# A fused attention and two-FFN kernel: the first token tile takes one chunk of each of the four batches instead of four chunks in a row, and its state products are issued after the first FFN products

## The chip, the core and the metric

The kernel runs on one core of a Trainium2 chip. The core has five engines with a queue each, and each queue is worked off in order: TensorE (PE: matmuls, and PEld, its weight loads), VectorE (DVE), ScalarE (ACT), GpSimd (POOL) and SyncE (SP). In this kernel SP issues every DMA, in the order in which the program names them. The metric is the device time of the program in microseconds, the median of several runs.

## The reference, cut to what matters

```python
batch, n_heads, seq, head_dim, d_state = (4, 8, 768, 32, 16)
for c in range(nc):                      # attention, chunk by chunk along the sequence
    cum = np.cumsum(la, axis=-1)         # la = log(clip(a))
    L = np.exp(cum[:, :, :, None] - cum[:, :, None, :]) * causal
    y_intra = einsum('bhij,bhjd->bhid', einsum('bhin,bhjn->bhij', Cc, Bc) * L, xc)
    y_inter = einsum('bhin,bhnd->bhid', Cc, state) * exp(cum)
    y[:, :, sl] = y_intra + y_inter
    state = decay_full * state + sum_j(Bc x xc * decay_from_j)
x = y as (3072 tokens, 256)              # token = batch * 768 + position
x = square(relu(x @ w_in)) @ w_out       # first FFN, width 2048
out = ((x @ w1) * (x @ w2)) @ w3 @ w_out2   # second FFN, width 1024
```

The state begins at zero in each batch, so the first chunk of a batch has no `y_inter`. The weights come as 64-bit floats.

## The kernel before, in words

**Tiles, chunks, units.** The chunk on the chip is 128 positions, so a batch has `NCH` = 6 chunks and all four have 24, numbered g = 0 to 23. A tile t is `CPT` = 4 chunks, 512 tokens, and there are 6 tiles. Before the change g runs along a batch first: chunks 0 to 5 are batch 0, and tile 0 holds its first four. A unit is two neighbouring chunks of a tile, for which `unit_load` brings B and C in one transfer (`raw`).

**Attention of a chunk.** `decays_e` makes, by a product of a mask matrix (`m_rel`) with the split logarithms (`la_r`) and an exponential, the rows of decay factors, 16 chunks to a call. `decays_e_out` writes them to DRAM (`e_d`); `chunk_e` reads those of a chunk back in four transfers of 128 KB, each row spread over 32 partitions, into the tile `e`. `chunk_g0` makes B C^T of a chunk of tile 0 (products L428) out of C as `unit_pad` spreads it by DVE or ACT (L395, `cp`); `chunk_m0` multiplies it into `e` (L441). `chunk_xb` loads x and B (`xb`, 256 KB), and `chunk_pre` scales both halves of it by decays on POOL (L382, `dec_in` for x, `dec_after` for B). `chunk_y` gives the chunk's outputs: 8 products with `e` (L497) and, if the batch has a state by then, 8 with the state and the scaled C (L502, operand `d`, made by `unit_scale` from `d_d`, which `decays_d_out` wrote to DRAM). ACT and DVE then split the outputs into the two parts of `xt` (L510 and L102), on which the FFNs work. A chunk's contribution to the state is 8 small products (`chunk_ds`, L450); `chunk_s` adds it to the decayed state before it (L466, L469). For the later tiles a chunk's products with B come from parts that go through DRAM (`hl_d`, read back as `bt` and `cb`; products L408, L412).

**FFNs.** Phase A of a tile is 16 blocks: `h_mm` (6 products, L519), ACT relu (L531), a square (L539), its split into two parts (`gp`, ACT L547 and DVE L102), and 6 products into the accumulator (`x2_mm`, L564). Phase B is the second FFN, in 8 blocks. The order is A0, A1, B0, B1, A2, B2 and so on, with the attention of the next tile put between the blocks by a table of slots (`put`, `slot`).

**Weights.** 16 pieces `ua` of 512 KB bring w_in and w_out of a block each. A piece becomes two float32 parts by two passes of ACT (L157, L159), two of DVE (L168, L171) and a split (ACT L188, DVE L102): `steps`. The block m of phase A0 cannot begin before piece m is converted.

**Order.** What runs ahead of phase A0 is written out by hand at the end of the function, with constants that place loads (`LOADS`, `DOUT`, `ULOAD`, `USPLIT`) and conversions (`INN`, `PADPOS`). A scheduler that goes by a model of durations then orders the compute engines' instructions; the DMAs keep the program's order. A pool's tile that is asked for again waits for the last reader of its buffer.

## Time and profile before

| | us |
|---|---|
| time, median of 3 runs | 596.36 |
| the three runs | 595.3, 596.36, 601.17 |
| span of the profiled execution, first to last instruction | 594.5 |
| PE busy in it | 566.4 |
| DVE busy | 345.9 |
| ACT busy | 291.8 |
| POOL busy | 66.6 |

The profile is one execution more, whose own device time is not listed; its span of 594.5 us lies 0.8 us under the fastest run and 1.9 us under the median. In what follows a time within the span is counted from the first instruction. PE is the engine that the whole is built around (95% of the span), but the share is a mean over a start of some 70 us, in which it waits often, and a remainder in which it hardly waits.

### The profile page before, as it was taken

How to read it: one execution, taken by the hardware profiler on the slowest of the kernel's cores; microseconds unless marked ns; L12 is line 12 of the kernel's file. 1: busy time of each engine (PE TensorE's matmuls, PEld its weight loads, DVE VectorE, ACT ScalarE, POOL GpSimd, SP SyncE). 2: the span in 40 equal slices, each digit the busy share in tenths (PEclk: the TensorE clock that was granted, in tenths of full speed). 3: DMA queues.
4: the chain of work that ended last, by engine and by line, in shares of the span. 5: the costliest groups of instructions: out<-in, count | busy, mean ns of one | idle time of the engine just before them, and what ended most of it. 6: DMA issues, size and time to landing. Idle time of an engine off the chain costs nothing.

```text
span 594.5 us, 9516 instructions
## 1 busy us (share of the span) xinstructions
PE 566.4 (95%) x3636; PEld 451.9 (76%) x3636; DVE 345.9 (58%) x593; ACT 291.8 (49%) x542; POOL 66.6 (11%) x77
## 2 busy tenths in 40 slices
PE   6687899899999999999999999999999999999997
PEld 4254577688988887888777888678888678888786
DVE  5668688887789654456454466354457353445332
ACT  6377788897765332444333444323444233444331
POOL 4302140000003030022030030030030020000000
PEclk9679999999999999999999999999999999999999
DMA  7998995143367260070250170340260320100001
GB/s 227 247 330 232 258 365 222 36 143 107 106 225 200 89 175 14 36 203 1 93 148 1 49 191 6 109 128 1 80 160 35 102 60 1 36 1 0 1 0 37
DMA packets 39165, 66.23 MB, mean 111 GB/s; under 512 B 4944, under 2 KB 23120, under 8 KB 39120
## 3 DMA queue, kind: packets, MB, share of 16 engines
q1 hardware_dynamic: 39120, 65.63, 36.8%
q8 instruction: 29, 0.48, 0.4%
q14 instruction: 16, 0.13, 0.1%
HBM read 55.12 MB, written 10.49 MB: 110 GB/s over the span
## 4 chain that ended last, share of the span: by engine, by line
PE 80%; DMA 11%; ACT 3%; DVE 3%; SPq 1%; issue 1%; DVEq 0%; ACTq 0%
PE mm L519 40%; PE acc L564 18%; PE acc L612 12%; PE mm L215 4%; DMA bt<-hl_d 2%; PE y L497 2%; DMA d<-d_d 2%; DMA e<-e_d 2%; PE y L502 2%; PE g L408 1%; SPq L88 1%; DMA u<-in_w_dram 1%; DMA ua<-in_w_dram 1%; PE y L450 1%; DMA xb<-in_xb_dram 1%
## 5 line engine op out<-in xcount | busy, mean ns | idle before, releaser
L564 PE MATMUL acc<-gp,wa 128*128 128x512 f32 x576 | 148.7, 394 | 5.1 <-ACT gp L547 4.8
L519 PE MATMUL mm<-xt,wa 128*128 128x512 f32 x576 | 148.6, 397 | 2.1 <-DVE wa L102 1.1
L547 ACT CAST gp<-tmp 128x512 fp32r<-128x512 f32 x144 | 89.4, 621 | 119.9 <-DVE tmp L603 69.5
L519 PE MATMUL mm<-x,w 128*128 128x512 f32 x576 | 144.4, 395 | 1.2 <-ACT tmp L595 0.7
L102 DVE TENSOR_TENSOR gp<-tmp,gp 128x512 fp32r<-128x512 f32 x144 | 103.9, 722 | 69.3 <-ACT gp L547 69.0
L564 PEld LDWEIGHTS acc<-gp,wa 128*128 128x128 f32 x576 | 105.4, 188 | 29.6 <-ACT gp L547 6.9
L519 PEld LDWEIGHTS mm<-xt,wa 128*128 128x128 f32 x576 | 107.2, 191 | 25.8 <-DVE wa L102 2.1
L519 PEld LDWEIGHTS mm<-x,w 128*128 128x128 f32 x576 | 104.1, 188 | 23.7 <-issue 1.8
L531 ACT ACTIVATE tmp<-mm 128x512 f32<-128x512 f32 x96 | 57.2, 596 | 52.5 <-PE mm L519 52.2
L612 PEld LDWEIGHTS acc<-w3o,gp 128*128 128x128 f32 x576 | 75.5, 190 | 4.6 <-issue 1.0
L612 PE MATMUL acc<-w3o,gp 128*128 128x256 f32 x576 | 78.3, 283 | 0.0
L382 POOL TENSOR_TENSOR xb<-xb,dec_in 128x256 f32<-128x256 f32 x24 | 20.1, 838 | 399.0 <-DMA xb<-in_xb_dram 271.1
L541 DVE TENSOR_TENSOR tmp<-tmp 128x512 f32<-128x512 f32 x64 | 45.8, 716 | 30.2 <-ACT tmp L531 29.9
L603 DVE TENSOR_TENSOR tmp<-tmp,mm 128x512 f32<-128x512 f32 x48 | 32.8, 683 | 45.7 <-PE mm L519 39.2
L595 ACT COPY tmp<-mm 128x512 f32<-128x512 f32 x48 | 27.7, 586 | 42.4 <-PE mm L519 42.4
L414 DVE TENSOR_TENSOR e<-g,e 128x512 f32<-128x512 f32 x40 | 26.8, 686 | 26.3 <-POOL e L372 22.2
L372 POOL TENSOR_SCALAR_AFFINE_SELECT e<-e 128x1024 f32<-128x1024 f32 x20 | 24.8, 1240 | 18.5 <-DMA e<-e_d 16.6
L497 PE MATMUL y<-e,xb 128*32 128x128 f32 x384 | 24.2, 299 | 2.3 <-DVE e L441 1.5
L215 PE MATMUL mm<-wo,w 128*128 128x256 f32 x128 | 23.4, 282 | 0.0
L510 ACT CAST xt<-y 128x128 fp32r<-128x128 f32 x48 | 12.5, 264 | 22.2 <-DVE xt L102 10.2
L215 PEld LDWEIGHTS mm<-wo,w 128*128 128x128 f32 x128 | 20.7, 191 | 1.0
L539 ACT ACTIVATE tmp<-tmp 128x512 f32<-128x512 f32 x32 | 20.2, 632 | 0.3
(84 smaller groups left out, 418.7 us busy)
## 6 DMA issues: line engine op xcount, KB each, us to landing
e<-e_d SPq DMA_DIRECT2D x96, 128.0 KB, 3.8
u<-in_w_dram SPq DMA_DIRECT2D x24, 512.0 KB, 4.3
ua<-in_w_dram SPq DMA_DIRECT2D x16, 512.0 KB, 6.3
xb<-in_xb_dram SPq DMA_DIRECT2D x24, 256.0 KB, 3.7
hl_d<-gp SPq DMA_DIRECT2D x8, 512.0 KB, 2.8
bt<-hl_d SPq DMA_DIRECT2D x30, 128.0 KB, 2.9
cb<-hl_d SPq DMA_DIRECT2D x60, 64.0 KB, 2.6
raw<-in_raw_dram SPq DMA_DIRECT2D x12, 256.0 KB, 4.1
```

The source lines that it names most:

```text
L102: return nc.vector.tensor_tensor(out=lo, in0=src, in1=hi.bitcast(F32), op=ALU.subtract)
L215: nc.tensor.matmul(acc[:, :DM], v[:, l, e % 4 * P:(e % 4 + 1) * P], wo2[1 + e // 2][r][:, e % 2 * DM:(e % 2 + 1) * DM], start=(n == 0), st ...
L414: nc.vector.tensor_tensor(out=m, in0=ps, in1=m, op=ALU.mult)
L497: nc.tensor.matmul(ys[32 * q:32 * q + 32, hg], ch["xb"][:, 0, h, :], ch["e"][:, h, :], start=True, stop=(c == 0))
L519: nc.tensor.matmul(ps, w[m][:, l, col + k * P:col + (k + 1) * P], rhs[k][:, r, :], start=((l, r, k) == (1, 0, 0)), stop=((l, r, k) == (0, ...
L531: nc.scalar.activation(r, ps, AF.Relu)
L541: nc.vector.tensor_tensor(out=g32, in0=r, in1=r, op=ALU.mult)
L547: nc.scalar.copy(g[:, 0, :], d[k])
L564: nc.tensor.matmul(acc["x2", t][e], wa[m][:, l, 256 + e * P:256 + (e + 1) * P], g[:, r, :], start=(m == 0 and n == 0), stop=(m == MF - 1 a ...
L595: nc.scalar.copy(s, ps)
L603: nc.vector.tensor_tensor(out=p32, in0=prods[t, m], in1=ps, op=ALU.mult)
L612: nc.tensor.matmul(acc["o"][sub // 2][:, sub % 2, :], g[:, l, sub * P:(sub + 1) * P], w3o[m // 2][:, r, m % 2, :], start=(m == 0 and n == ...
```

## The change: what it does

- Chunk g is now chunk g // 4 of batch g % 4. Tile t holds the t-th chunk of each batch, so tile 0 is the four first chunks, which have no state: its `chunk_y` has no L502 products. Every chunk of tiles 1 to 5 has them. The states are four tiles, one per batch, updated in place.
- Since batches lie in other places of the inputs, `unit_load` makes two transfers (512-byte pieces) of what was one, the logarithms are reordered as they are clipped (`la_in` to `la`, the unused columns set by POOL), and the output rows are picked per batch.
- `chunk_xb` of tile 0 loads x first (128 KB) and B by a second transfer (`chunk_xb_half`); `chunk_pre` of it scales x first and B later.
- The state products of tile 0 (`states_0`) come after the outputs of its chunks, and `decays_d_out(0)`, which wrote 256 KB for chunks 0 to 3, now writes those of chunks 4 to 7, later; `unit_load_d` and `unit_scale` of units 0 and 1 go.
- The written-out order ahead of phase A0 is replaced, and with it the constants.

In tiles 1 to 5 the same slots hold the same calls as before. Line numbers of the changed kernel differ: L88 becomes L89, L263 L272, L395 L422, L428 L455, L450 L477, L497 L513, L519 L536, L564 L581.

```diff
+GB = NB
...
-    dec_d = wts.tile([P, 2 * P], F32, tag="w123", name="dec_d")
+    dec_d = const.tile([P, 2 * P], F32, name="dec_d")
     e_d = [dram.tile([4, LG, H, P], F32, name=f"e_d{i}") for i in range(2)]
-    d_d = [dram.tile([n, H, N, P], F32, name=f"d_d{n}") for n in (4, 12, 8)]
+    d_d = [dram.tile([n, H, N, P], F32, name=f"d_d{k}") for k, n in enumerate((4, 8, 8))]
     m_raw = new_tmp()
     m_rel = tmp.tile([P, 512], F32R, tag="tmp", name="m_rel")
     m_oth = new_tmp()
+    la_in = new_tmp()[:, :2 * LG * H]
...
-        nc.vector.tensor_scalar(out=la, in0=la, scalar1=1e-6, scalar2=1.0, op0=ALU.max, op1=ALU.min)
+
+        n = NG * H
+        nc.vector.tensor_scalar(
+            out=la[:, :n].rearrange("p (k b h) -> p k b h", k=NCH, b=NB),
+            in0=la_in[:, :n].rearrange("p (b k h) -> p k b h", k=NCH, b=NB),
+            scalar1=1e-6, scalar2=1.0, op0=ALU.max, op1=ALU.min,
+        )
+        nc.gpsimd.memset(la[:, n:], 1.0)
...
-        r0, n, i = ((0, 4, 0), (32, 12, 0), (0, 8, 1))[k]
+        r0, n, i = ((32, 4, 0), (64, 8, 0), (0, 8, 1))[k]
...
-        dma(out=raw, in_=raw_in[u].rearrange("p (s t) -> p s t", s=2))
+        k, b0 = divmod(u * CPU, NB)
+        for j in range(CPU):
+            part = raw_in[(b0 + j) * (S // UT) + k // CPU].rearrange("p (s t) -> p s t", s=2)
+            dma(out=raw[:, :, j * P:(j + 1) * P], in_=part[:, :, k % CPU * P:(k % CPU + 1) * P])
         units[u] = {"raw": raw}
...
-    state = {}
+    state = [const.tile([P, 2, D], F32, name=f"s{b}") for b in range(NB)]
+
+    def tokens(g):
+
+        r0 = g % NB * S + g // NB * P
+        return slice(r0, r0 + P)
 
     def chunk_xb(g, place=None):
         if place:
             xb = wts.tile([P, 2, H, D], F32, tag=place, name="xb")
         else:
             xb = at.tile([P, 2, H, D], F32, tag="xb", name="xb")
-        dma(out=xb.rearrange("p s h d -> p (s h d)"), in_=xb_in[g * P:(g + 1) * P, :])
         chs[g] = {"xb": xb}
+        if g < GB:
+            chunk_xb_half(g, 0)
+        else:
+            dma(out=xb.rearrange("p s h d -> p (s h d)"), in_=xb_in[tokens(g), :])
+
+    def chunk_xb_half(g, s):
+        n = H * D
+        dma(
+            out=chs[g]["xb"][:, s].rearrange("p h d -> p (h d)"), in_=xb_in[tokens(g), s * n:(s + 1) * n]
+        )
...
-    def chunk_pre(g):
+    def chunk_pre(g, parts=(0, 1)):
         ch = chs[g]
         k0 = g * H
         if g >= CPT:
             causal(ch["e"])
-        for s, dec in enumerate((dec_in, dec_after)):
+        for s in parts:
+            dec = (dec_in, dec_after)[s]
...
-        """The state after chunk g, from the one before it."""
-        c = g % NCH
-        if g < CPT - 1:
-            if c == 0:
-                state["0"] = wts.tile([P, CPT - 1, 2, D], F32, tag="wa11", name="s0")
-            s = state["0"][:, c]
-        elif g == CPT - 1 or c == 0:
-            s = at.tile([P, 2, D], F32, tag="s", name="s", bufs=1)
-        else:
-            s = state[g - 1]
-        if c == 0:
+
+        u, j = divmod(g, CPU)
+        s = state[g % GB]
+        if g < GB:
             nc.vector.tensor_copy(s, ds)
         else:
-            u, j = divmod(g, CPU)
             nc.vector.scalar_tensor_tensor(
-                out=s, in0=state[g - 1], scalar=units[u]["dl"][:, j:j + 1], in1=ds, op0=ALU.mult, op1=ALU.add,
+                out=s, in0=s, scalar=units[u]["dl"][:, j:j + 1], in1=ds, op0=ALU.mult, op1=ALU.add,
             )
-        state[g] = s
...
-        own = g >= CPT and c < NCH - 1
+        own = 0 < ti < NCH - 1
         if own:
             chunk_ds(g, yp[:, :, P:P + D])
         for hg in range(2):
             for q in range(4):
                 h = 2 * q + hg
                 nc.tensor.matmul(
-                    ys[32 * q:32 * q + 32, hg], ch["xb"][:, 0, h, :], ch["e"][:, h, :], start=True, stop=(c == 0)
+                    ys[32 * q:32 * q + 32, hg], ch["xb"][:, 0, h, :], ch["e"][:, h, :], start=True, stop=(ti == 0)
                 )
-            for q in range(4 if c > 0 else 0):
+            for q in range(4 if ti > 0 else 0):
                 rows = slice(32 * q, 32 * q + 32)
                 nc.tensor.matmul(
-                    ys[rows, hg], state[g - 1][rows, hg, :], cs[rows, j, :], start=False, stop=True
+                    ys[rows, hg], state[sub][rows, hg, :], units[u]["cs"][rows, j, :], start=False, stop=True
                 )
         if own:
             chunk_s(g, yp[:, :, P:P + D])
-        del chs[g]
+        if ti > 0:
...
+    def states_0():
+        ds = new_mm()[:, :CPT * 2 * D].rearrange("p (g k d) -> p g k d", g=CPT, k=2)
+        for g in range(CPT):
+            chunk_ds(g, ds[:, g])
+        for g in range(CPT):
+            chunk_s(g, ds[:, g])
+            del chs[g]
...
     unit_load(0)
     decays_ln()
+    chunk_xb(0)
     unit_load(1)
-    chunk_xb(0)
+    chunk_xb(1)
     conv_load(1)
     decays_e(0)
     decays_e_out(0)
-    decays_d()
-    if DOUT == 0:
-        decays_d_out(0)
-    chunk_xb(1)
     decays_cols()
+    for g in range(2, CPT):
+        chunk_xb(g, f"w12{4 + g}")
     unit_pad(0, 0, "wa15")
     unit_pad(0, 1, "wa14")
-    if PADPOS == 0:
-        unit_pad(1, 0, "wa13")
-        unit_pad(1, 1, "wa12")
     chunk_g0(0)
-    steps(1, False, False)
+    chunk_e(0)
+    chunk_e(1)
     chunk_g0(1)
-    if PADPOS == 1:
-        unit_pad(1, 0, "wa13")
-        unit_pad(1, 1, "wa12")
-    chunk_e(0)
-    if DOUT == 0:
-        unit_load_d(0)
-        unit_load_d(1)
-    chunk_e(1)
-    if DOUT == 1:
-        decays_d_out(0)
-        unit_load_d(0)
-        unit_load_d(1)
-    for g in range(2, CPT):
-        chunk_xb(g, f"w12{4 + g}")
-    conv_load(LOADS[0])
-    decays_e(1)
+    chunk_e(2, "w124")
+    chunk_e(3, "w125")
+    conv_load(2)
+    unit_pad(1, 0, "wa13")
+    unit_pad(1, 1, "wa12")
     chunk_g0(2)
     chunk_g0(3)
-    chunk_e(2, "w124")
-    conv_load(LOADS[1])
-    chunk_e(3, "w125")
-    conv_load(LOADS[2])
-    decays_e_out(1)
-    decays_d_out(1)
-    decays_d_out(2)
-    decays_e_out(2)
-    unit_scale(0)
-    unit_scale(1)
-    ds = new_mm()[:, :CPT * 2 * D].rearrange("p (g k d) -> p g k d", g=CPT, k=2)
+    steps(1, False, False)
     for g in range(CPT):
-        chunk_pre(g)
+        chunk_pre(g, (0,))
+    decays_d()
+    decays_e(1)
     for g in range(CPT):
-        chunk_ds(g, ds[:, g])
-    for g in range(CPT):
-        chunk_s(g, ds[:, g])
-    for g in range(CPT):
-        for _ in range(INN[g]):
-            steps(1, False, at_piece[0] < sum(INN))
         chunk_m0(g)
         chunk_y(g)
-        if g == ULOAD:
+        if g == 0:
+            for i in range(CPT):
+                chunk_xb_half(i, 1)
+            conv_load(1)
+            decays_d_out(0)
             unit_load(2)
             unit_load(3)
-            conv_load(LOADS[3])
-        if g == USPLIT:
-            unit_split(2, "w120")
-            unit_split(3, "w121")
-    for _ in range(INN[CPT]):
-        steps(1, False, at_piece[0] < sum(INN))
+            conv_load(2)
+        if g < 3:
+            steps(1, False, at_piece[0] < 3)
+    unit_split(2, "w120")
+    unit_split(3, "w121")
+    for g in range(CPT):
+        chunk_pre(g, (1,))
+    states_0()
+    decays_e_out(1)
     unit_load_d(2)
     unit_load_d(3)
     chunk_e(4)
     unit_bc(2)
     chunk_e(5)
-    conv_load(LOADS[4])
+    conv_load(1)
+    decays_e_out(2)
+    decays_d_out(1)
+    decays_d_out(2)
```

How this moves instructions, first on PE at the start of the program (`mm<-m_rel,la_r` is the product behind the decay rows, `g` that of B and C, `mm<-xb` the state products, `y` the outputs). Before:

```order
L263 MATMUL mm<-m_rel,la_r 128x512 x2
L284 MATMUL d<-tmp 128x128 x2
L278 MATMUL mm<-tmp 128x192 x2
L263 MATMUL mm<-m_rel,la_r 128x512 x2
L428 MATMUL g<-cp,raw 128x512 x4
L450 MATMUL mm<-xb 32x32 x8
L428 MATMUL g<-cp,raw 128x512
```

After:

```order
L455 MATMUL g<-cp,raw 128x512 x2
L272 MATMUL mm<-m_rel,la_r 128x512
L455 MATMUL g<-cp,raw 128x512 x2
L272 MATMUL mm<-m_rel,la_r 128x512
L287 MATMUL mm<-tmp 128x192 x2
L455 MATMUL g<-cp,raw 128x512 x2
L272 MATMUL mm<-m_rel,la_r 128x512 x2
L455 MATMUL g<-cp,raw 128x512 x2
L293 MATMUL d<-tmp 128x128 x2
L513 MATMUL y<-e,xb 32x128 x32
L477 MATMUL mm<-xb 32x32 x8
L536 MATMUL mm<-xt,wa_227 128x512
```

The first two products for the decay rows stood at the head of the queue; now four products `g` stand ahead of the second of them.

The start of DVE's queue (the first row clips the logarithms; `m_rel` and `la_r` are the operands of the product behind the decay rows; `cp` is the spread C). Before:

```order
L250 TENSOR_SCALAR tmp<-tmp 128x256
L255 CAST m_rel<-tmp 128x512
L102 TENSOR_TENSOR la_r<-tmp,la_r 128x256
L395 TENSOR_SCALAR cp<-raw,tmp 128x256 x12
L168 SCALAR_TENSOR_TENSOR cvs<-cvs,ua_121 128x512
```

After:

```order
L254 TENSOR_SCALAR tmp<-tmp 128x192
L422 TENSOR_SCALAR cp<-raw,tmp 128x256 x7
L264 CAST m_rel<-tmp 128x512
L422 TENSOR_SCALAR cp<-raw,tmp 128x256
L103 TENSOR_TENSOR la_r<-tmp,la_r 128x256
L422 TENSOR_SCALAR cp<-raw,tmp 128x256 x4
```

The cast of `m_rel` and the split of `la_r` moved behind seven and eight of the instructions that spread C.

SP's queue from the first decay rows (`e_d<-tmp`) on (`d_d` and `d` are the decays for the state products, `ua` and `u` weights, `raw` B and C, `hl_d` the parts of B and C). Before:

```order
L88 DMA e_d_94<-tmp 32x4x128
L88 DMA d_d_96<-dec_d 512x1x128
L88 DMA xb<-in_xb_dram 128x512
L88 DMA e<-e_d_94 32x1024 x4
L88 DMA d_188<-d_d_96 128x2x128
L88 DMA d_190<-d_d_96 128x2x128
L88 DMA e<-e_d_94 32x1024 x4
L88 DMA xb<-in_xb_dram 128x512 x2
L88 DMA e<-e_d_94 32x1024 x4
L88 DMA ua_227<-in_w_dram 128x1024
L88 DMA e<-e_d_94 32x1024 x4
L88 DMA ua_234<-in_w_dram 128x1024
```

After:

```order
L89 DMA e_d_94<-tmp 32x4x128
L89 DMA xb<-in_xb_dram 128x256 x2
L89 DMA e<-e_d_94 32x1024 x16
L89 DMA ua_193<-in_w_dram 128x1024
L89 DMA ua_195<-in_w_dram 128x1024
L89 DMA xb<-in_xb_dram 128x256 x4
L89 DMA ua_262<-in_w_dram 128x1024
L89 DMA d_d_96<-dec_d 512x1x128
L89 DMA raw<-in_raw_dram 128x2x128 x4
L89 DMA ua_271<-in_w_dram 128x1024
L89 DMA ua_273<-in_w_dram 128x1024
L89 DMA hl_d_341<-hl 128x2x512
```

The 16 reads of decay rows now stand in one block, the three weight pieces that stood between and right behind them stand behind it, and two reads of `d` and one write of `d_d` are gone from the head. Further on, the larger writes of `d_d` and the last of `e_d`, which stood ahead of pieces `ua` 4 to 7, stand between pieces 6 and 7.

## Rows read from the trace of the kernel before

**Rows 1.** Busy time by stretch: PE, PEld, DVE, ACT, POOL, clock, DMA share, GB/s.

```profile
9.70:69.20 59.50, 45.01 (x338) 25.86 (x337) 42.15 (x75) 37.40 (x76) 12.33 (x16) 0.86 0.94 260
48.00:58.00 10.00, 6.80 (x44) 4.75 (x43) 8.44 (x14) 7.16 (x14) 4.28 (x5) 1.00 0.74 194
66.00:70.00 4.00, 1.78 (x11) 1.25 (x10) 3.40 (x8) 3.90 (x8) 0.00 (x0) 1.00 0.61 163
70.00:80.00 10.00, 10.00 (x76) 7.54 (x75) 6.66 (x12) 8.74 (x18) 4.88 (x5) 1.00 1.01 309
120.00:594.50 474.50, 469.13 (x2973) 385.58 (x2971) 256.51 (x429) 205.15 (x374) 42.30 (x48) 1.00 0.27 80
```

**Rows 2.** The chain of waits, in order of time: start, length, what.

```profile
6.81 2.82 DMA e_d<-tmp
...
57.66 9.17 DMA bt<-hl_d
```

**Rows 3.** Timeline, DVE from the start: start, length, instruction, wait before it.

```profile
4.04 0.77 DVE L255 CAST m_rel<-tmp 128x512 fp32r<-128x512 f32 x1 [0.40 <-DMA tmp<-in_masks_dram]
4.73 0.40 DVE L102 TENSOR_TENSOR la_r<-tmp,la_r 128x256 fp32r<-128x256 f32 x1
6.29 3.24 DVE L395 TENSOR_SCALAR cp<-raw,tmp 128x256 f32<-128x256 f32 x12 [1.15 <-DMA raw<-in_raw_dram]
```

**Rows 4.** Timeline, PE from the start (a float32 product counts as two).

```profile
4.96 1.19 PE L263 MATMUL mm<-m_rel,la_r 128*128 128x512 f32 x2 [4.96 <-DVE m_rel L255]
...
8.93 4.26 PE L428 MATMUL g<-cp,raw 128*128 128x512 f32 x8
```

**Rows 5.** Timeline, from the first exponential to the first read of decay rows.

```profile
6.19 0.60 ACT L265 ACTIVATE tmp<-mm 128x512 f32<-128x512 f32 x1
...
8.18 0.61 SPq L88 DMA_DIRECT2D xb<-in_xb_dram  x1
...
9.69 1.73 SPq L88 DMA_DIRECT2D e<-e_d  x4
```

**Rows 6.** Timeline, tile 0's first blocks and the wait for unit 3.

```profile
32.75 6.83 PE L519 MATMUL mm<-xt,wa 128*128 128x512 f32 x18 [0.52 <-ACT xt L510]
...
37.73 0.62 ACT L105 CAST hl<-raw 128x512 fp32r<-128x512 f32 x1 [2.74 <-DMA raw<-in_raw_dram]
...
39.29 0.59 ACT L531 ACTIVATE tmp<-mm 128x512 f32<-128x512 f32 x1
...
68.99 0.41 PE L412 MATMUL g<-cb,bt 96*128 96x128 f32 x2 [2.22 <-DMA cb<-hl_d]
```

**Rows 7.** Timeline, PE: chunk 6 without a state, chunk 7 with one.

```profile
81.50 0.33 PE L450 MATMUL y<-xb 128*32 128x32 f32 x16
...
82.31 2.59 PE L564 MATMUL acc<-gp,wa 128*128 128x512 f32 x10
...
92.25 0.33 PE L450 MATMUL y<-xb 128*32 128x32 f32 x16
...
93.91 1.65 PE L564 MATMUL acc<-gp,wa 128*128 128x512 f32 x6
```

**Rows 8.** Busy time by stretch, columns as in the first group.

```profile
20.00:22.00 2.00, 0.44 (x16) 0.31 (x16) 0.64 (x2) 0.27 (x1) 2.00 (x3) 0.62 1.08 234
...
38.00:40.00 2.00, 1.65 (x8) 1.03 (x7) 1.28 (x2) 1.56 (x4) 0.00 (x0) 1.00 1.02 402
44.00:46.00 2.00, 0.17 (x1) 0.17 (x2) 1.97 (x5) 2.00 (x5) 0.00 (x0) 1.00 1.06 381
```

**Rows 9.** Timeline, PE: the wait during which the clock fell.

```profile
21.54 0.44 PE L450 MATMUL mm<-xb 128*32 128x32 f32 x16 [2.86 <-POOL xb L382]
```

**Rows 10.** The page's DMA issues: count, size of each, us to landing.

```profile
raw<-in_raw_dram SPq DMA_DIRECT2D x12, 256.0 KB, 4.1
...
d<-d_d SPq DMA_DIRECT2D x12, 128.0 KB, 3.8
...
d_d<-dec_d SPq DMA_DIRECT2D x1, 256.0 KB, 3.3
```

More of the change, by code (lines that the diff above doesn't have):

```diff
@@ L242, in decays_load @@
         if k == 0:
-            dma(out=la, in_=a)
+            dma(out=la_in, in_=a)
         elif k == 1:
@@ L306, in unit_load_d @@
         g = u * CPU
-        k = 0 if g < 4 else 1 if g < LG else 2
-        g -= (0, 4, LG)[k]
+        k = 0 if g < 8 else 1 if g < LG else 2
+        g -= (4, 8, LG)[k]
         dma(out=d4, in_=d_d[k][g:g + CPU].rearrange("c h n i -> (h n) c i"))
@@ L454, in chunk_s @@
     def chunk_s(g, ds):
-        c = g % NCH
-        if g < CPT - 1:
-            if c == 0:
-                state["0"] = wts.tile([P, CPT - 1, 2, D], F32, tag="wa11", name="s0")
-            s = state["0"][:, c]
-        elif g == CPT - 1 or c == 0:
-            s = at.tile([P, 2, D], F32, tag="s", name="s", bufs=1)
-        else:
-            s = state[g - 1]
-        if c == 0:
+        u, j = divmod(g, CPU)
+        s = state[g % GB]
+        if g < GB:
             nc.vector.tensor_copy(s, ds)
         else:
-            u, j = divmod(g, CPU)
             nc.vector.scalar_tensor_tensor(
-                out=s, in0=state[g - 1], scalar=units[u]["dl"][:, j:j + 1], in1=ds, op0=ALU.mult, op1=ALU.add,
+                out=s, in0=s, scalar=units[u]["dl"][:, j:j + 1], in1=ds, op0=ALU.mult, op1=ALU.add,
             )
-        state[g] = s
     def chunk_y(g):
-        c = g % NCH
         ch = chs[g]
         u, j = divmod(g, CPU)
-        cs = units[u]["cs"]
         ti, sub = divmod(g, CPT)
@@ L625, in out_evac @@
                 nc.scalar.copy(o, acc["o"][j])
-            r0 = t * TT + 2 * j * P
-            dma(out=out[r0:r0 + 2 * P, :].rearrange("(s p) e -> p s e", p=P), in_=o)
+            rows = out.rearrange("(b k p) e -> k p b e", b=NB, k=NCH)[t]
+            dma(out=rows[:, 2 * j:2 * j + 2, :], in_=o)
     PHASES = [("A", 0), ("A", 1), ("B", 0), ("B", 1)] + [(ph, t) for t in range(2, NTILE) for ph in "AB"]
@@ L698, in attention_plan_1 @@
         put(ph, BCSLOT, unit_bc, 3, BCPLACE)
+    def states_0():
[4 more added lines that the diff above has]
+            chunk_s(g, ds[:, g])
+            del chs[g]
     attention_plan_1()
```

## Prediction

> **What bounds the kernel now.** I first read the busy time by stretch [rows 1]. From 120 us to the end PE is busy 469.1 of 474.5 us, so there an instruction more or less on PE is time more or less, and nothing else is. The start is different. From 9.7 to 69.2 us PE is busy 45.0 of 59.5 us, and the DMA engines have a share of 0.94 at 260 GB/s: SP's loads, in their written order, are the fullest resource. From 70 to 80 us PE is busy all the time. So the handover from loads to PE lies near 69 us, and the timeline shows it: PE's last long wait, 2.22 us, ends at 68.99 with the landing of `cb` of unit 3 [rows 6]. The chain of waits agrees: it runs from the decay rows' write at 6.81 through DMAs to `bt` of that unit, issued at 57.66 and waited for 9.17 us later [rows 2]. What the change is worth at the start is therefore how much earlier or later that landing comes, not how much earlier the first FFN product does. The latter is hidden anyway: the first three blocks' products were issued from 32.75 on, but ACT, whose queue held the split of unit 2 and 3 ahead of the first relu, waited for `raw` and came to that relu at 39.29 [rows 6].
>
> Times below are within the profiled span of 594.5 us; the median of the runs lies 1.9 us above it, and I add that at the end.
>
> **Term 1, the decay rows leave later.** The queue of loads can't run on before the decay rows are written and read back. Before, both masks' products stood first on PE, at 4.96, the exponential began at 6.19, and the reads of the rows at 9.69 [rows 4, 5]. In the changed order DVE spreads C seven times before it casts `m_rel`, an eighth time before it splits `la_r`, and PE has two products `g` ahead of each of the two. DVE can begin when `raw` lands, 6.29; a spread takes 3.24/12 = 0.27 us [rows 3]. Four give the first `g` at 7.37; seven, the cast (0.77), the eighth and the split (0.40) end at 9.62. On PE a `g` takes 4.26/4 = 1.07 us and a mask product 1.19/2 = 0.60 [rows 4]: 7.37, two `g` to 9.50, a mask product to 10.10, two `g` to 12.23, the other to 12.83. The exponential thus starts 6.6 us later than at 6.19. If the `g` cost PE nothing, DVE alone would make it 9.62 + 0.60, 4.0 us later; if PE took twice as long for its first two `g`, 8.7 us. I take +6.6: every piece of it is a row of the same instruction. The clip of the logarithms now also waits for a fill on POOL, and `raw` comes in 512-byte pieces by twice as many transfers. The fill has until 6.29, since DVE waits for `raw` anyway, and costs nothing. For the pieces the nearest row is `d`, whose 128 KB also move in 512-byte pieces and take 3.8 us to landing, against 4.1 for a `raw` of 256 KB [rows 10]. Two such at once cost nothing more, two in turn 3.5 us; I take nothing, since they are issued one behind the other without a wait, and leave the rest to the range.
>
> **Term 2, the loads get shorter.** Between 9.7 and 69.2 us some 260 x 59.5 = 15.5 MB move [rows 1]. The change removes one 256 KB write of `d_d` and two reads of `d` of 128 KB [rows 10], 0.52 MB. Chunk 1's `xb`, 256 KB, was issued at 8.18 and can't have landed by 9.7, since even the 64 KB of `e_d` took 2.82 [rows 2, 5]; now the x halves of all four chunks, which together are twice that, are loaded while the rows are awaited, and only the B halves, 0.52 MB as the two `xb` that came later before, stand behind them. That is another 0.26 MB out of the stretch. 0.78 MB at 260 GB/s are 3.0 us. Every other load ahead of unit 3's `cb` stands ahead of it still, in another order.
>
> **Term 3, holes in the queue.** In 48 to 58 and 66 to 70 us the share is 0.74 and 0.61 [rows 1]: 0.26 x 10 + 0.39 x 4 = 4.2 us in which the DMA engines had nothing to do, because reads of `bt`, `cb` and `e` wait for writes. A reordered queue may fill all of that or none. The waits themselves remain, so I take half, 2.1 us.
>
> Sum for the handover: 6.6 - 3.0 - 2.1 = +1.5 us, between 4.0 - 3.0 - 4.2 = -3.2 and 8.7 - 3.0 = +5.7. At the handover about as much of phase A0 is done as before: the order puts one chunk more of tile 1 ahead of it and one or two blocks' second products behind.
>
> **Term 4, the state products come back where PE is full.** Tile 0 loses the L502 products of three chunks. They lay in the start, between landings, and give nothing. But chunks 6, 12 and 18, which began a batch and had none, now have them, in tiles 1, 3 and 4. A chunk with a state takes 93.91 - 92.25 = 1.66 us of PE, one without 82.31 - 81.50 = 0.81 [rows 7]: 0.85 us each, 2.55 us for the three, 1.7 if the one in tile 1 falls into a wait. I take 2.5. The state increments themselves (L450) change places but not number: 20 chunks before and after. What DVE and POOL are spared (the scaling of two units) lies in a stretch where DVE is busy 42.2 of 59.5 us [rows 1] and costs and gives nothing; if DVE were the bound there it would give under 1 us. The two-piece transfers of the later tiles and the output rows, still 1 KB long, lie under 474 us in which the DMA share is 0.27 [rows 1].
>
> **Sum.** 594.5 + 1.5 + 2.5 = 598.5 us of span, 600.4 us as a median.
>
> **Rival 1: the start, not the queue, sets phase A0 (faster).** If A0's pace is that of ACT and DVE from the landing of `raw` of unit 3, then what counts is the bytes ahead of it. The writes of `d_d` for 20 chunks (64 KB each) and of `e_d` (448 KB) stood ahead of it; now only 4 chunks' `d_d` does. With the 0.52 MB of term 2 that is 2.0 MB less, 7.7 us at 260 GB/s. With the rows 6.6 us late, that leaves -1.1 us: 594.5 - 1.1 + 2.5 + 1.9 = 597.8. If the rows were not late at all, because `raw` lands early and the first products of PE are quick, -7.7 gives 591.2, and with some of the holes filled under 590. For it speaks that ACT did wait for `raw` just ahead of the first relu [rows 6]; against it, the wait for `cb` 30 us later, which no earlier start removes.
>
> **Rival 2: TensorE's clock falls in a new hole (slower).** Weight piece 6 stood right behind the `raw` of unit 3; now about 3.9 MB more stand ahead of it (`hl_d` 1.05, `e` of two chunks 1.05, `bt` and `cb` 0.79, two `xb` 0.52, `d` 0.26, `e_d` 0.2), 15 us at 260 GB/s, and three more writes ahead of piece 7. Blocks 0 to 5 run dry meanwhile, so PE gets a hole of some 5 us, an estimate, with little but a chunk's products in it. The granted clock fell to a mean of 0.62 in 20 to 22 us, in which PE waited 2.86 us [rows 8, 9]; FFN products ran from 32.75, and the clock was full again in 38 to 40 [rows 6, 8]: 5.3 us at half clock, which costs 2.6 us of a stretch where PE is full. In 44 to 46 us PE was busy only 0.17 us and the clock stayed at 1.00 [rows 8], so a hole must be longer than that one, or have less ahead of it. Price: 600.4 + 2.6 = 603.0, with the upper end of term 1 up to 606. It decides if PE gets no FFN product for longer than in the stretch around 45 us. By the Trainium skill (TensorE: Matmul & The Clock Gate, section Why this matters for your kernels), idle gaps between bursts of matmuls take the engine back to half clock, and sustained work releases it. By that the hole would give 603.0; the trace agrees at 20 us and not at 45 us.
>
> **Rival 3: the first product isn't earlier.** On PE the state products of tile 0 stand between the first block's products and wait for the B halves. That holds back a product whose relu waits for `raw` anyway, so it gives the forecast's 600.4.
>
> **How the numbers follow.** About 1% (6 us) is what a measurement of this kernel can tell from no change: 590.4 to 602.3. The forecast has 0.57 with rival 3 in it, rival 1 0.13, rival 2 0.30. Of rival 1 half lies under 590.4. Of rival 2 most lies above 602.3, and of the forecast's own spread (-3.2 to +5.7 around +1.5) a sixth. So faster 0.07, same 0.58, slower 0.35. The range leaves out the far halves of both rivals: 592 to 606.
>
> **What would show it.** Term 1: the first read of decay rows issued near 16 us, not 9.7, and a stretch with a low DMA share before it. Terms 2 and 3: the landing of `cb` of unit 3 near 70.5 us. Term 4: PE busy about 1.7 us more from tile 2 on. Rival 1: full PE from well before 65 us. Rival 2: a granted clock under 1.00 after 50 us. The prediction is wrong if the reads begin before 12 us, or if PE fills up long before unit 3's `cb` lands.

## The result and the profile after

The changed kernel took 602.39 us, median of 4 runs (601.18 to 604.47); the kernel before took 597.33 in the 4 runs beside it (595.3 to 601.17). The ratio is 1.010 with a 95% interval of 1.007 to 1.014. The prediction was 600.4 us, from a median of 596.36 at that time: it expected 4.0 us more, and 5.1 came. The profiled execution of after has a span of 599.5 us, 5.0 more than before. It is the fastest of the four (601.18 us) and has the highest mean clock, 0.983; the other three have 0.971 to 0.973, and what their starts look like is not on record.

Where the 5.0 us lie is seen at the first relu of phases A2, A3 and A4, which both kernels come to with the same blocks behind them. ACT's timeline, before (columns: start, duration, then engine, line, operation, operands, and in brackets the idle time before it and what ended it):

```profile
245.84 0.60 ACT L531 ACTIVATE tmp<-mm 128x512 f32<-128x512 f32 x1 [1.47 <-PE mm L519]
...
333.42 0.60 ACT L531 ACTIVATE tmp<-mm 128x512 f32<-128x512 f32 x1 [1.47 <-PE mm L519]
...
420.89 0.60 ACT L531 ACTIVATE tmp<-mm 128x512 f32<-128x512 f32 x1 [1.47 <-PE mm L519]
```

and after:

```profile
249.19 0.60 ACT L548 ACTIVATE tmp<-mm 128x512 f32<-128x512 f32 x1 [1.47 <-PE mm L536]
...
337.60 0.60 ACT L548 ACTIVATE tmp<-mm 128x512 f32<-128x512 f32 x1 [1.47 <-PE mm L536]
...
426.01 0.60 ACT L548 ACTIVATE tmp<-mm 128x512 f32<-128x512 f32 x1 [1.47 <-PE mm L536]
```

A2 begins 3.35 us later. From A2 to A3 it is 88.41 us after and 87.58 before, from A3 to A4 88.41 and 87.47: 0.83 and 0.94 us more. The rest, some 173.5 us to the end, is equal within 0.2. So the start cost 3.35 us, and the attention of tiles 3 and 4 cost 1.8.

Up to the start of A2 the time can be split into PE's work and PE's waits. The windows show both (columns: stretch, length, busy time and count of PE, its weight loads, DVE, ACT, POOL, then the granted clock, the DMA share and GB/s), before and after:

```profile
0.00:245.84 245.84, 222.60 (x1513) 172.64 (x1514) 176.90 (x317) 158.42 (x302) 34.48 (x41) 0.97 0.59 180
0.00:249.19 249.19, 220.62 (x1513) 172.92 (x1514) 175.99 (x315) 158.51 (x303) 35.59 (x42) 0.96 0.57 176
```

PE waits 28.57 us instead of 23.24, 5.33 more, and works 1.98 us less, since tile 0 has no state products and tile 1 has one chunk's more. So it is the waits that made the start longer.

The start first, in ACT's and SP's timelines, where the exponential and the first read of the decay rows stand that answer to [rows 5]:

```profile
14.31 0.60 ACT L274 ACTIVATE tmp<-mm 128x512 f32<-128x512 f32 x1 [6.96 <-PE mm L272]
```

```profile
16.61 0.80 SPq L89 DMA_DIRECT2D e<-e_d  x2
```

The exponential starts 8.1 us later than the 6.19 of before, the first read 6.9 us later than 9.69. The windows show what the queue did meanwhile and behind that (columns as above; the clock of 1.00 in the first row is no measurement, as the last section explains):

```profile
9.70:16.40 6.70, 6.70 (x17) 3.32 (x15) 3.16 (x6) 2.08 (x6) 1.18 (x2) 1.00 0.06 13
16.40:71.74 55.34, 38.88 (x329) 25.02 (x327) 38.04 (x67) 36.16 (x74) 12.82 (x15) 0.81 0.93 272
58.00:60.00 2.00, 0.82 (x14) 0.41 (x10) 1.41 (x4) 0.88 (x3) 0.00 (x0) 1.00 1.07 296
60.00:62.00 2.00, 0.00 (x0) 0.00 (x0) 1.46 (x4) 0.78 (x2) 0.00 (x0) 0.66 0.94 232
62.00:64.00 2.00, 1.78 (x4) 1.49 (x5) 0.36 (x2) 0.00 (x0) 0.00 (x0) 0.50 0.99 356
64.00:66.00 2.00, 2.00 (x31) 0.87 (x33) 0.69 (x1) 1.95 (x4) 0.00 (x0) 0.50 0.99 381
66.00:68.00 2.00, 1.66 (x24) 0.50 (x24) 1.94 (x4) 2.00 (x5) 0.00 (x0) 0.63 1.07 308
68.00:70.00 2.00, 1.30 (x6) 1.05 (x6) 1.97 (x5) 2.00 (x5) 0.00 (x0) 1.00 0.89 194
70.00:80.00 10.00, 7.61 (x51) 5.65 (x50) 7.15 (x13) 8.79 (x19) 2.31 (x3) 1.00 0.93 276
80.00:100.00 20.00, 20.00 (x155) 14.75 (x154) 17.92 (x34) 16.94 (x33) 4.37 (x4) 1.00 1.02 367
...
120.00:599.50 479.50, 473.76 (x3012) 388.72 (x3010) 261.04 (x431) 207.44 (x379) 42.86 (x48) 1.00 0.27 79
```

6.7 us with a DMA share of 0.06, then 55 us at 272 GB/s. In 60 to 62 us PE does nothing at all, and the granted clock, 1.00 in 58 to 60, goes to its lower level (0.50, 1.2 GHz) and is back at 68. PE's and ACT's timelines tell what it waited for:

```profile
57.38 0.69 ACT L158 ACTIVATE cvs<-ua 128x512 f32<-128x512 f32 x1 [5.18 <-DMA ua<-in_w_dram]
```

```profile
58.32 0.50 PE L435 MATMUL g<-cb,bt 96*128 96x256 f32 x2
62.22 2.93 PE L536 MATMUL mm<-xt,wa 128*128 128x512 f32 x6 [3.40 <-DVE wa L103]
65.08 0.44 PE L477 MATMUL y<-xb 128*32 128x32 f32 x16
...
68.70 1.65 PE L536 MATMUL mm<-xt,wa 128*128 128x512 f32 x6 [1.04 <-DVE wa L103]
71.18 0.41 PE L439 MATMUL g<-cb,bt 96*128 96x128 f32 x2 [0.82 <-DMA cb<-hl_d]
...
79.16 0.33 PE L477 MATMUL y<-xb 128*32 128x32 f32 x16 [1.32 <-POOL xb L409]
```

Weight piece 6 landed at 57.36 (43.17 before), its conversion ended at 62.2, and block 6 could not begin earlier. PE's wait for `cb` of unit 3, which [rows 6] shows at 68.99, is now at 71.18. And it is not the last one: chunk 6 makes PE wait at 79.16, and 70 to 80 us hold 7.61 us of PE work, where [rows 1] has 10.00. Behind that PE is busy 20.00 of 20 us, so 79.16 is the last wait for a landing that PE has in the start. The chain of waits that ended last goes on past it (start, duration, what):

```profile
61.36 7.83 DMA bt<-hl_d
69.20 0.86 SPq L89
...
73.87 8.54 DMA xb<-in_xb_dram
82.55 0.86 POOL xb L409
...
84.68 1.55 POOL e L398
...
86.86 0.68 DVE cvs L169
87.65 0.69 DVE wa L103
88.33 0.60 DVE cvs L172
```

It stays in SP's queue until 82.4 us, when `xb` of chunk 7 lands, goes through POOL to `e` of that chunk, and then to DVE, which has the product with `e` and the conversions of the next pieces in one queue. What these later links cost is not seen, as PE is busy meanwhile.

### The profile page after: what moved, and what is told of

Same layout as the page of the kernel before. It is cut to its first block, busy times and chain, and to the rows that moved or that the text cites. A ratio compares the mean times of both kernels' runs of the same rounds, so it can differ in the third digit from the quotient of the medians.

```text
span 599.5 us, 9540 instructions
## 1 busy us (share of the span) xinstructions
PE 566.0 (94%) x3636; PEld 452.2 (75%) x3636; DVE 347.5 (58%) x589; ACT 291.8 (49%) x542; POOL 67.5 (11%) x78
## 4 chain that ended last, share of the span: by engine, by line
PE 79%; DMA 10%; SPq 3%; ACT 3%; DVE 3%; issue 1%; POOL 0%; DVEq 0%; ACTq 0%; POOLq 0%
PE mm L536 39%; PE acc L581 18%; PE acc L629 12%; PE mm L216 4%; SPq L89 3%; DMA raw<-in_raw_dram 3%; DMA xb<-in_xb_dram 2%; PE y L513 2%; DMA bt<-hl_d 2%; PE y L518 2%; PE g L435 1%; PE g L455 1%; DMA ua<-in_w_dram 1%; DMA e_d<-tmp 1%; PE y L477 1%
## 5 line engine op out<-in xcount | busy, mean ns | idle before, releaser
L536 PE MATMUL mm<-xt,wa 128*128 128x512 f32 x576 | 150.1, 398 | 5.1 <-DVE wa L103 5.1
L581 PE MATMUL acc<-gp,wa 128*128 128x512 f32 x576 | 147.8, 394 | 4.3 <-ACT gp L564 4.0
L564 ACT CAST gp<-tmp 128x512 fp32r<-128x512 f32 x144 | 89.4, 621 | 120.8 <-DVE tmp L620 70.4
L536 PE MATMUL mm<-x,w 128*128 128x512 f32 x576 | 144.6, 395 | 1.6 <-ACT tmp L612 1.1
L103 DVE TENSOR_TENSOR gp<-tmp,gp 128x512 fp32r<-128x512 f32 x144 | 105.9, 736 | 68.3 <-ACT gp L564 67.7
L536 PEld LDWEIGHTS mm<-xt,wa 128*128 128x128 f32 x576 | 107.4, 191 | 27.4 <-DVE wa L103 6.2
L581 PEld LDWEIGHTS acc<-gp,wa 128*128 128x128 f32 x576 | 105.6, 188 | 28.4 <-ACT gp L564 5.6
L536 PEld LDWEIGHTS mm<-x,w 128*128 128x128 f32 x576 | 103.9, 188 | 24.2 <-issue 2.0
L558 DVE TENSOR_TENSOR tmp<-tmp 128x512 f32<-128x512 f32 x64 | 47.3, 739 | 29.7 <-ACT tmp L548 29.2
L409 POOL TENSOR_TENSOR xb<-xb,dec_in 128x256 f32<-128x256 f32 x24 | 18.3, 767 | 393.8 <-DMA xb<-in_xb_dram 383.1
L513 PE MATMUL y<-e,xb 128*32 128x128 f32 x384 | 25.0, 305 | 7.1 <-DVE e L468 5.1
L513 PEld LDWEIGHTS y<-e,xb 128*32 128x32 f32 x384 | 10.2, 116 | 17.5 <-issue 16.2
```

The source lines that it names most:

```text
L103: return nc.vector.tensor_tensor(out=lo, in0=src, in1=hi.bitcast(F32), op=ALU.subtract)
L513: nc.tensor.matmul(ys[32 * q:32 * q + 32, hg], ch["xb"][:, 0, h, :], ch["e"][:, h, :], start=True, stop=(ti == 0))
L536: nc.tensor.matmul(ps, w[m][:, l, col + k * P:col + (k + 1) * P], rhs[k][:, r, :], start=((l, r, k) == (1, 0, 0)), stop=((l, r, k) == (0, ...
L558: nc.vector.tensor_tensor(out=g32, in0=r, in1=r, op=ALU.mult)
L564: nc.scalar.copy(g[:, 0, :], d[k])
L581: nc.tensor.matmul(acc["x2", t][e], wa[m][:, l, 256 + e * P:256 + (e + 1) * P], g[:, r, :], start=(m == 0 and n == 0), stop=(m == MF - 1 a ...
```

## The experiments

"After" is 602.39 us or 1.0103 of before; every ratio below is to the runs of the kernel before beside it (medians 596.66 to 597.47), with its 95% interval. The interval of after itself, from 4 runs, is 1.007 to 1.014; those of e2, e3, f2, f3 and f4 overlap with it, that of e1 ends at its edge, and h2, h3 and h4 lie clear of it. "The mark" is the relu of block 8 of A1 (counted from 0), at 136.19 before and 139.50 after in the profiled executions, a measure of the start's length. One execution is a rough measure: f4 has the order of after on every engine throughout the start, and its A2 begins at 251.77 instead of 249.19, 2.6 us later. Smaller differences of a mark show nothing by themselves. Landings are those of the single transfers in the trace.

### e1: decay rows first

```diff
-        nc.vector.tensor_copy(m_rel, m_raw)
+        keep(nc.vector.tensor_copy(m_rel, m_raw))
...
     for l in range(2):
-        nc.tensor.matmul(ps, la_r[:, l, i * P:(i + 1) * P], m_rel, ...)
+        mm = nc.tensor.matmul(ps, la_r[:, l, i * P:(i + 1) * P], m_rel, ...)
+        if i == 0:
+            keep(mm)
```

and the same `keep` (the program's order is the engine's) for the split of `la_r`, the spreads of unit 0, chunk 0's `g`, and tile 0's `y` and state products behind them.

> Changed kernel with the split of the logarithms, the cast of m_rel and the two mask products put ahead of the spreading of C and of the products g on DVE and PE, so that the decay rows leave as early as before the change; the scheduler's order behind it shifts with that. Changed kernel: 602.4 us, first read of rows 16.61, cb of unit 3 landed 71.74. If the queue of loads sets the start (the prediction's term 1): first read near 9.7, cb of unit 3 near 65, time near 596, 0.998 of the kernel before. Rival (the hole ahead of block 6 and the clock in it cost the time, and early rows only fill an idle stretch of the DMA engines): the hole stays as long, time 600 to 602.

599.71 us, ratio 1.004 (1.002 to 1.007). The first read left at 10.92 instead of 16.61, but `cb` of unit 3 landed only 2.9 us earlier, at 68.81: the share was 0.80 in 38 to 46 us and 0.66 in 62 to 68. In its profiled execution, which took 600.99 us, the mark stands at 139.50, as after. So early rows alone are worth 0.6% at the medians and not 1.1%: half of their lead of 5.7 us was lost by the landing of `cb`, with new holes in the queue. Neither theory had that. Half clock did not go, but lay at 42 to 45 and 69 to 72 us instead of 61 to 67.

### e2: pieces 6 and 7 earlier

```diff
             unit_load(3)
-            conv_load(2)
+            conv_load(4)
...
     chunk_e(5)
-    conv_load(1)
```

> Changed kernel with weight pieces 6 and 7 loaded right behind pieces 4 and 5, ahead of hl_d, e, bt and cb of tile 1 (16 and 12 DMA issues earlier). The bytes ahead of cb of unit 3 stay the same. If the queue's length sets the start: cb of unit 3 lands at 71.7 as before and the time stays at 602.4 (within 0.6). If the hole of 3.4 us ahead of block 6 and the half clock behind it cost the time (the prediction's rival 2): no half clock after 58 us, time 598.8 to 600, by the 2.6 us that the rival was priced at or by the whole 3.3 us that the start is longer.

601.50 us, ratio 1.008 (1.005 to 1.011): 0.9 us less than after at the medians, within the intervals. Blocks 6 and 7 ran at once, and then PE waited 2.29 us, up to 66.42, for chunk 5's part of `xt` and came to block 8 at 69.04, whose piece landed at 64.02 (the 68.2 that the expectations of h2 name is piece 10's landing); the clock was at 0.63 and 0.52 in 66 to 70 us. So this run has half clock too, and tells nothing of its price. The rows of chunk 7 landed at 84.17 (84.60 after). The hole had moved, and the bytes ahead of `cb` of unit 3, which landed at 71.91, had not changed.

### e3: 1.31 MB of writes later

```diff
-    decays_e_out(2)
-    decays_d_out(1)
-    decays_d_out(2)
...
     attention_plan_1()
+    put(("A", 0), 14, decays_e_out, 2)
+    put(("A", 0), 14, decays_d_out, 1)
+    put(("A", 0), 14, decays_d_out, 2)
```

> Changed kernel with three writes (d_d of chunks 8 to 23, 1.05 MB, and e_d of chunks 16 to 23, 0.26 MB) moved from between pieces 6 and 7 to block 7 of phase A0. They stand ahead of pieces 7 to 10 and of cb of unit 3, behind piece 6. If the queue's length sets the start: 1.31 MB at 279 GB/s are 4.7 us, cb of unit 3 at 67.0, time near 598. If the hole ahead of block 6 does: piece 6 lands at 57.4 as in the changed kernel, half clock behind it as there, time 601.5 to 602.4.

600.33 us, ratio 1.005 (1.003 to 1.008). Piece 6 landed at 57.87 and the hole grew to 5.85 us, with half clock behind it as after, yet the time fell by 2.1 us. That speaks for the bytes and against the hole, though the intervals overlap. `cb` of unit 3 landed at 68.17, 3.6 us earlier than after and 1.05 earlier than before the change, and yet the mark, at 138.03, is 1.8 us later than before. Why, is seen in PE's windows from its wait for `cb` to A2, before and in e3:

```profile
68.99:245.84 176.85, 173.06 (x1165) 142.99 (x1166) 129.90 (x228) 115.76 (x219) 16.82 (x18) 1.00 0.47 151
68.14:247.47 179.33, 175.96 (x1223) 145.50 (x1224) 130.63 (x231) 117.00 (x222) 16.72 (x18) 1.00 0.50 156
```

PE waits 3.37 us there, no more than the 3.79 of before, but has 2.9 us more work left: 42 products of the blocks' first kind (L536) were done by then, 7 blocks, where before had 48 (L519), 8 blocks, and chunk 6's state products come on top. The hole, in which PE went dry, had cost what the early landing gave. DVE has a long wait behind that:

```profile
77.70 1.29 DVE L441 TENSOR_TENSOR e<-g,e 128x512 f32<-128x512 f32 x2 [4.29 <-POOL e L398]
```

It waits 4.29 us for chunk 6's rows, which landed at 76.42 and went through POOL, with conversions of weight pieces queued behind it. f2 and h4 try what these rows are worth.

### f2: rows of chunks 6 and 7 ahead of pieces 12 and 13; f3: e3 and f2

```diff
-        put(ph, 8, chunk_xb, 6, "w124")
-        put(ph, 8, chunk_e, 6, "w122")
-        put(ph, 9, chunk_xb, 7, "w125")
-        put(ph, 9, chunk_e, 7, "w123")
+        put(ph, 5, chunk_xb, 6, "w124")
+        put(ph, 5, chunk_e, 6, "w122")
+        put(ph, 5, chunk_xb, 7, "w125")
+        put(ph, 5, chunk_e, 7, "w123")
```

> Changed kernel with xb and decay rows of chunks 6 and 7 loaded ahead of weight pieces 12 and 13. By the waits of the runs so far (DVE waits 2 to 4 us near 78 us for the decay rows of chunk 6, with the conversions of pieces 11 and 12 queued behind) these landings set the second half of phase A0: they come 1.9 and 3.8 us earlier, time 599 to 600.5. Rival (pieces 12 and 13, now later by as much, set it): no difference, 602.4. If the prediction's handover at cb of unit 3 were the last bound: no difference either, with full PE from 73 us on.

> Both e3 (1.31 MB of writes later) and f2 (rows of chunks 6 and 7 ahead of pieces 12 and 13). If the bytes ahead of the rows of chunks 6 and 7 set the start: those rows land near 74.5 and 78, earlier than in the kernel before (75.7, 80.3), and the start is no longer than before, so the time is that of the kernel before and 1.7 to 2.5 us for the state products, 598.5 to 599.5. If the half clock ahead of that sets it: as e3, 600.3.

f2: 600.49 us, ratio 1.007 (1.005 to 1.010), 1.9 us less than after; the rows landed at 78.28 and 81.99 instead of 79.39 and 84.60, and DVE's long wait near 80 us is down to 0.99 (2.10 after), with new ones of up to 1.98 us for weight pieces. In its profiled execution the granted clock was 0.53 from 60 to 78 us, and A2 begins 0.5 us earlier than after: up to there PE waits 4.6 us less and its work, with the same products, takes 4.1 us longer (224.72 and 220.62). f3: 600.30 us, 1.005 (1.003 to 1.008), no better than e3, although the rows landed at 73.32 and 78.20: pieces 12 and 13 came at 79.23 and 80.50, and half clock lay at 64 to 74 us. So f3 came out at the rival's time: with the hole in place, fewer bytes and another order don't add. Whether the clock is the reason, as the rival has it, or the later pieces, isn't shown.

### e5 and f4: without the state products

```diff
-            for q in range(4 if ti > 0 else 0):
+            for q in range(4 if ti > 0 and g not in (6, 12, 18) else 0):
```

In f4 the list is (12, 18). In both the `stop` of these chunks moves to their products with `e`.

> Changed kernel without the state products (L518) of chunks 6, 12 and 18, the three that had none in the kernel before; their outputs lack the state's part. Term 4: three times 0.85 us of a full PE, time 2.5 us less, 599.9; 1.7 us less, 600.7, if the one in tile 1 lies in a wait. Rival (PE has room for them): no difference.

> Changed kernel without the state products (L518) of chunks 12 and 18 alone (tiles 3 and 4; their outputs lack the state's part); PE's order is otherwise that of the changed kernel. Term 4: two times 0.85, 1.7 us less, 600.7, with A2 to B3 shorter by 0.85 each and the start unchanged. Rival: the time stays, 602.4.

f4: 600.81 us, ratio 1.007 (1.004 to 1.009), 1.6 us less than after, 1.7 expected. From A2 to A3 and from A3 to A4 it is 87.57 us each, where after has 88.41: 0.84 a chunk. That, and not the median, is what shows the cost, since in the same execution the start, which has the order of after, was 2.6 us longer, with half clock at 45.6, 62.6, 69.5 and 76.3 us. e5: 602.84 us (1.010, 1.007 to 1.014), no gain. It has the gain in the tiles (87.58 and 87.88), but leaving out chunk 6's eight products changed the order that the scheduler made of the start, and A2 began 5.0 us later than after in its profiled execution, with a clock of 0.61 in 60 to 80 us; how much of that is the order is open. What the state products cost in tile 1 is therefore not shown.

### f1 and h1: products of no use in the hole

```diff
+            if (t, m) == (0, 6):
+                ps = new_mm()
+                for _ in range(8):
+                    keep(nc.tensor.matmul(ps, wa[0][:, 0, 0:P], xt[0][0][:, 0, :], start=True, stop=True))
             h_mm(t, m)
```

and `keep` for the first products of blocks 5 and 6. In h1 there are three, float32, behind chunk 5's last product with B, reading its finished `e`.

> Changed kernel with eight products of no use put on PE ahead of the first product of block 6 (the scheduler also puts chunk 5's products ahead of them), to fill the hole of 3.4 us that ends at 62.22 there. Rival 2's price (half clock behind the hole lengthens the path): granted clock 1.00 from 60 to 68 us, time 2.6 us less, 599.8. Rival (landings of cb of unit 3 at 71.7 and of the decay rows of chunks 6 and 7 at 79.4 and 84.6 set the path, the slow products lie inside them): the clock stays up, those landings and the time stay, 602.4 within 0.6.

> Changed kernel with three products of no use (128x512, float32, an estimate of 0.85 us each) on PE between chunk 5's second product with B and the first product of block 6, in the hole that ended at 62.22; they read chunk 5's finished e, so nothing else waits for them, and PE's order is otherwise nearly that of the changed kernel. If the half clock behind the hole is on the path: clock 1.00 from 60 to 68 us and 2 to 3 us less, 599.4 to 600.4. If the landings of the decay rows of chunks 6 and 7 (79.4, 84.6) set the path whatever the clock does: 602.4 within 0.6.

Both were slower: 608.69 us (1.020, 1.017 to 1.023) and 604.13 us (1.012, 1.009 to 1.014). In f1 chunk 5's products came to stand ahead of block 6 and waited 3.21 us for `xt`, so the hole stayed. In h1 the useless products began at 60.83, after 1.6 us without work. PE's windows in h1:

```profile
58.00:60.77 2.77, 1.23 (x22) 0.61 (x18) 1.71 (x5) 1.48 (x3) 0.00 (x0) 1.00 1.04 274
60.77:64.19 3.42, 3.36 (x4) 1.51 (x5) 1.65 (x4) 0.78 (x2) 0.00 (x0) 0.50 1.02 287
64.19:71.01 6.82, 4.90 (x61) 2.76 (x60) 4.24 (x8) 5.42 (x10) 0.00 (x0) 1.00 0.91 269
71.01:77.84 6.83, 5.80 (x18) 4.44 (x17) 5.22 (x10) 4.92 (x11) 0.00 (x0) 0.50 0.70 249
```

The clock fell all the same, at 60.77, just ahead of the first of them; it was back at 64.19 (67.48 after) and fell again at 71.01. The products took 4.47 us where 2.6 was the estimate, and block 6 began at 64.75 instead of 62.22. Neither run kept the clock up, so neither tells what the fall costs.

### h2, h4 and h3: putting the order right

h2 is e2 and e3, h4 is h2 and f2, h3 is h2 and e1.

> e2 and e3 together: pieces 6 and 7 loaded right behind piece 5, and 1.31 MB of writes moved behind piece 15. e2 alone only moved the hole to block 8 (piece 8 landed at 68.2), e3 alone kept it ahead of block 6. Together piece 8 should land at 58 to 60, when blocks 6 and 7 are just done: no hole and no half clock after 40 us, cb of unit 3 near 68. Then the start is as long as before the change and the time is that of the kernel before and 2.5 us for the state products: 599 to 599.7, or a little less. If the two only act on the same bound: as e3, 600.3.

> h2 and f2 together (rows of chunks 6 and 7 also ahead of pieces 12 and 13). If DVE's wait for these rows is the last bound once the hole is gone: they land near 74 and 78, time 597.5 to 598.5. If pieces 12 and 13, now later, are: as h2.

> h2 and e1 together (decay rows leave first as well). In e1 the rows left 6.9 us earlier and cb of unit 3 landed only 2.9 us earlier, since new waits took the rest. If that holds on top of h2: cb of unit 3 near 65, start 2 to 3 us shorter than in h2, time 596 to 597.5, as fast as the kernel before or a little faster. Rival (the order of PE shifts so that new holes and half clock appear): 599 to 601.

h2: 598.74 us, ratio 1.002 (1.000 to 1.004). h4: 596.11 us, 0.999 (0.997 to 1.001). h3: 593.74 us, 0.995 (0.993 to 0.997), faster than both kernels. h4 and h3 came out faster than their expectations. (The 6.9 us that the one of h3 gives for e1's rows are 5.7.) h4 is the test of the rows of chunks 6 and 7: against h2 they landed at 73.87 and 76.84 instead of 75.98 and 81.41, while `cb` of unit 3 came 0.7 us later (68.88) and half clock was as long; the time fell by 2.6 us (12 runs each), A2 in the two traces by 1.1. h2 and h3 differ in nothing but the decay rows' place and what the scheduler makes of it. Windows of h2:

```profile
38.00:60.00 22.00, 19.57 (x99) 15.00 (x98) 18.21 (x33) 19.15 (x35) 4.71 (x6) 1.00 0.83 263
60.00:80.00 20.00, 17.00 (x131) 11.85 (x130) 13.38 (x24) 13.67 (x26) 4.53 (x6) 0.83 0.95 256
80.00:120.00 40.00, 35.79 (x242) 26.53 (x241) 34.45 (x61) 33.12 (x66) 2.42 (x2) 1.00 0.62 224
```

and of h3:

```profile
38.00:60.00 22.00, 17.48 (x112) 11.66 (x110) 18.53 (x30) 19.17 (x38) 6.38 (x6) 1.00 0.88 222
60.00:80.00 20.00, 18.35 (x166) 13.35 (x167) 15.31 (x27) 14.80 (x30) 5.52 (x6) 1.00 1.02 307
80.00:120.00 40.00, 37.75 (x220) 29.94 (x220) 33.75 (x62) 35.98 (x70) 0.00 (x0) 1.00 0.48 182
```

In h2 there is a hole still, 3.0 us ahead of `cb` of unit 3 at 68.14, and half clock behind it. In h3 the first read leaves at 10.94 (16.78 in h2), `cb` of unit 3 lands at 60.64 (68.19), the clock is 1.00 from 38 us on in the profiled execution, and the mark is here:

```profile
132.76 0.60 ACT L559 ACTIVATE tmp<-mm 128x512 f32<-128x512 f32 x1 [1.36 <-PE mm L547]
```

5.8 us before that of h2 (138.57), and 3.4 before that of the kernel before the change. Up to A2, in h2 and in h3:

```profile
0.00:247.52 247.52, 221.18 (x1513) 173.75 (x1514) 175.96 (x315) 158.07 (x302) 34.91 (x42) 0.96 0.57 177
0.00:241.52 241.52, 216.36 (x1513) 172.37 (x1514) 176.42 (x315) 157.27 (x302) 35.78 (x42) 0.98 0.58 181
```

Of the 6.0 us that A2 is earlier PE's waits are 1.2 and its work is 4.8, with the same number of products: PE worked 14.3 us at half clock in h2 and 5.7 in h3. So most of what the early rows give on top of h2 comes in this pair of executions by way of the clock.

## Why the prediction was right, point by point

Direction and range held; the forecast was 2.0 us low, of which 1.0 is the kernel before itself, whose median moved from 596.36 to 597.33 with one run more. 602.39 lies nearer to rival 2's 603.0 than to the forecast's 600.4, and just above the 602.3 up to which the prediction took a time for no change; the interval, 1.007 to 1.014, excludes no change. Terms 1 and 4 hold in mechanism. That the sum came so near owes something to luck: errors in terms 1 to 3 offset each other, and one wait was left out.

- **Term 1**, +6.6 us for the late decay rows: the first read came 6.9 us later (16.61, where 16.3 was expected). Two errors offset. The exponential was 8.1 us late, not 6.6, since PE's four `g` and two mask products took 6.84 us from 7.47 to 14.31, where the sum had 5.46: a `g` took 1.9 us at first and not the 1.07 of [rows 4], as the last section shows. That is close to the prediction's upper case of 8.7. DVE was even quicker than in the sum. The write of the rows then landed in 1.65 us instead of the 2.82 of [rows 2], since the queues were empty when it was issued. What it is worth on top of h2 is shown by h3: 5.0 us at the medians, most of it, in the traces, by way of the clock. With the holes in place (e1) it is worth half of that.
- **Terms 2 and 3**, -3.0 and -2.1: from the first read to `cb` of unit 3 it was 59.5 us before and 55.1 after, 4.4 less where 5.1 was expected. Apart they are not as forecast: 272 GB/s for 55.3 us are 15.1 MB, 0.4 less than the 15.5 of before and not 0.78, which is 1.6 us; the removed write of `d_d` had landed at 10.79 before, so most of it lay outside the stretch. The rest is a rate of 272 instead of 260 GB/s at an equal share (0.93 and 0.94): holes that were filled, as term 3 has it, are not seen. The sum of the three, +1.5, was +2.5: the landing is at 71.74 instead of 69.22.
- **The handover.** For the kernel before the reading holds: behind the wait for `cb` PE is busy 10.00 of the next 10 us [rows 1]. In the changed kernel it does not, and this is what the prediction left out: chunk 6's `xb`, landed at 77.03, makes PE wait once more, 1.32 us at 79.16, and 70 to 80 us hold 2.39 us of waits. Of the start's +3.35, 2.2 us are PE's later meeting with `cb` (71.18 instead of 68.99), 1.0 are more waits from there to A2 (4.79 us instead of 3.79), and the rest is work; the forecast had +1.5 and 0.8. That about as much of phase A0 is done at the handover held after the change (48 first products in both, 36 second ones instead of 40) and failed in e3, where `cb` came earlier than before the change and the start was still longer. The rows of chunks 6 and 7 are worth something too, as h4 shows; that they are the last bound is not shown.
- **Term 4**, +2.5, at least 1.7 in tiles 3 and 4: these two are 0.83 and 0.94 in the trace, and without them f4 has 0.84 less each. The third is in the start, and e5 failed to separate it.
- **Rival 1** is out: PE had its longest wait (3.40 us) where the rival wanted full PE.
- **Rival 2** came true as an event: piece 6 landed late, PE ran dry, the clock fell, from 60.7 to 67.5 us. In the profiled execution no price of it is to be seen ahead of the handover: behind the slow stretch PE waited 1.04 us for piece 7 and 0.82 us for `cb`, so faster products would have waited longer. Nor does it set after apart from before, where PE worked 12.9 us at half clock up to A2 and after 13.5. Where PE has no such waits half clock does cost: in h2, behind `cb`, 12 first products took 5.23 us at 69.88, in e3, at full clock, 2.98. What it cost in the other executions of after is open. For a price speak the 29 runs of the kernel before beside h3, of which the ten with a mean clock up to 0.978 have a median of 598.1 us and the 13 from 0.982 on 596.0, and the runs of f3: the two with 0.980 took 597.03 and 598.12 us, the five at 0.973 to 0.974 took 599.89 to 602.33. Against it speak the 12 runs of h3, whose fastest, 591.9 us, has the lowest clock of them, 0.978. A hole slows the clock and the time alike, so this doesn't settle it, and the two attempts to hold the clock failed.
- **Rival 3** holds: the first FFN product came at 32.16 (32.75 before), and the first relu, 37.16, still behind the split of `raw`.

So most of what was lost lay in the order written with the change: spreads ahead of the decay rows, piece 6 behind chunk 5's rows, and 1.3 MB of writes, not needed before tile 2, ahead of piece 7. With these put right (h3) the changed chunk order is 3.7 us faster than the kernel before, state products included. That its fewer bytes ahead of phase A0 are the reason is not shown: the kernel before, with its writes and pieces moved likewise, was not run.
